# Placing layernorm and transposes of two row chunks a few matmul groups earlier in a fused transformer block, and requesting their input earlier

## The chip, the cores and the metric

The kernel runs on one core of a Trainium2 chip. The metric is the device time of one execution in microseconds (us). A profiled execution also has a span (first to last instruction), which is about 2 us shorter than the device time. The mean granted TensorE clock, as a share of the full clock, is 1.000 except where the text says otherwise.

Engines are named as in the profile: PE is TensorE (matmul), PEld its weight load, DVE VectorE, ACT ScalarE, POOL GpSimd, SP the engine that issues every DMA of this kernel (SPq is its sequencer). Line L178 is a helper through which nearly every instruction is recorded, so groups are told apart by their tiles, `out<-in`.

## The reference

One sequence of 2048 rows, width 1024: an adaptive layernorm, linear attention with 32 heads, then a SwiGLU feed-forward with hidden width 3584, both with residuals.

```
mod = silu(c) @ w_mod -> sa, ca, ga, sb, cb, gb
h = layernorm(x) * (1 + ca) + sa
q, k, v = split(h @ wqkv);  pq, pk = phi(q), phi(k)      # phi(t) = (t+1 if t>0 else exp(t)) + 1e-6
o = (pq @ (pk^T v)) / (pq . sum(pk) + 1e-6)
x = x + ga * (o @ wo)
h = layernorm(x) * (1 + cb) + sb
x = x + gb * ((silu(h @ w_gate) * (h @ w_up)) @ w_down)
```

Only the first layernorm and the q and k projections matter here, about the first 130 us.

## The kernel before

The program is a list of operations; each engine takes its own in list order, and semaphore waits are derived from the data. The 2048 rows are four chunks of 512 (four tiles of 128 rows). For chunk `ch` TensorE computes 8 k groups and 8 q groups of 8 matmuls each. ScalarE and VectorE then empty the group's PSUM bank (the memory that TensorE writes to); this is called evacuation. Work for the *next* chunks is hung between these groups: `add(s1, g, f)` puts `f` behind group `g` of chunk 1, `s2` is chunk 2, `kside` the k half of chunk 0.

```python
HT = T("ht", 120 * KB, [128, 2, NDT, 512], BF16)   # two buffers: chunk ch uses ch % 2

def ln1_stats_ops(st): ...   # VectorE: 2 x bn_stats (0.64 us), 1 x bn_aggr, per 128-row tile
def ln1_rstd(ch): ...        # VectorE, then POOL pow
def ln1_xn(st): ...          # VectorE: x = (x - mean) * rstd, in place, 0.46 us
def th_dma(st): ...          # SP: DMA transpose of the tile into HT (one per tile)
def th_mod(ch, dt):          # scale and shift one of 8 slices of the transposed chunk, in place
    if dt % 2 == 0 or ch == 1: P.dve("tensor_scalar", out=HT[:, ch % 2, dt, :], ...)   # 0.40 us
    else:                      P.act("activation",    out=HT[:, ch % 2, dt, :], ...)   # 0.82 us

def chunk(ch, side):
    for gi in range(16):
        if gi < 8: k_group(ch, gi)       # 8 matmuls reading HT[:, ch % 2, 0..7, :], then
        else:      q_group(ch, gi - 8)   # phi_evac: ACT exp and relu; DVE min/add and sum, in pairs
        for f in side.get(gi, []): f()

# chunk 2 (tiles 8..11), prepared during chunk 1
for i in range(4): add(kside, i, lambda i=i: x_load(8 + i))          # request x
for i, f in enumerate(ops8_11): add(s1, (i * 5) // 12, f)            # 12 statistics operations
add(s1, 4, lambda: ln1_rstd(2))
for jj in range(4):
    add(s1, 6 + jj // 2, lambda jj=jj: ln1_xn(8 + jj))
    add(s1, 6 + jj // 2, lambda jj=jj: th_dma(8 + jj))
for i, dt in zip([10, 11, 11, 12, 12, 13, 13, 14], range(8)): add(s1, i, lambda dt=dt: th_mod(2, dt))
# chunk 3 (tiles 12..15)
for i in range(4): add(s1, 2 * i, lambda i=i: x_load(12 + i))
for i, f in enumerate(ops12_15): add(s1, 8 + (i * 7) // 12, f)
add(s1, 15, lambda: ln1_rstd(3))
for jj in range(4):
    add(s2, 1 + jj, lambda jj=jj: ln1_xn(12 + jj)); add(s2, 1 + jj, lambda jj=jj: th_dma(12 + jj))
for dt in range(8): add(s2, 7 + dt, lambda dt=dt: th_mod(3, dt))
# ... cut: modulation rows (macc, 1.2 us each on VectorE, chunk 2 groups 4..11), attention, feed-forward
```

(Shortened: `ops8_11` and `ops12_15` stand for lists built in loops.)

## Time and profile before

Before: 839.48 us (median of 4 runs, 839.27 to 839.64).

| of the profiled execution | |
|---|---|
| span | 837.6 us |
| TensorE busy | 99% |
| TensorE's waits after 27 us that the change can reach | two shown, 1.20 and 0.44 us |

The page's busy times and its chain of waits say that TensorE's order of work is the time:

```profile
PE 827.7 (99%) x4113; PEld 380.2 (45%) x4113; DVE 306.1 (37%) x673; ACT 203.0 (24%) x355; POOL 41.1 (5%) x52
PE 91%; DVE 4%; SPq 2%; DMA 2%; issue 1%; ACT 0%; DVEq 0%; ACTq 0%
```

TensorE's timeline from the end of start-up to the 16 small matmuls after chunk 3's third k group. Columns: start, duration, engine, line, operation, `out<-in`, shapes, count, and in brackets the idle time before and what ended it. Consecutive equal instructions are merged.

```profile
26.83 49.34 PE L178 MATMUL ps<-ht,wqk 128*128 128x512 bf16 x226
77.37 27.80 PE L178 MATMUL ps<-ht,wqk 128*128 128x512 bf16 x128 [1.20 <-DVE ht L178]
105.61 4.06 PE L178 MATMUL ps<-ht,wqk 128*128 128x512 bf16 x18 [0.44 <-DVE ht L178]
109.50 0.54 PE L178 MATMUL ps<-ones,mhl 128*128 128x1 bf16 x16
```

Two stops are shown, while chunk 2 and chunk 3 begin. Both end when a scale step (`ht<-ht`) is done. Rows of VectorE's timeline (its first and last scale step for chunk 2, then for chunk 3), of ScalarE's (first and last for chunk 2), and of the issuing engine's:

```profile
71.59 0.41 DVE L178 TENSOR_SCALAR ht<-ht,modcol 128x512 bf16<-128x512 bf16 x1 [4.73 <-DMA ht<-xres]
76.91 0.41 DVE L178 TENSOR_SCALAR ht<-ht,modcol 128x512 bf16<-128x512 bf16 x1
94.57 0.41 DVE L178 TENSOR_SCALAR ht<-ht,modcol 128x512 bf16<-128x512 bf16 x1 [1.50 <-DMA ht<-xres]
105.15 0.40 DVE L178 TENSOR_SCALAR ht<-ht,modcol 128x512 bf16<-128x512 bf16 x1
```

```profile
71.57 0.81 ACT L178 ACTIVATE ht<-ht,modcol 128x512 bf16<-128x512 bf16 x1 [2.71 <-DMA ht<-xres]
76.56 0.84 ACT L178 ACTIVATE ht<-ht,modcol 128x512 bf16<-128x512 bf16 x1
```

```profile
60.82 2.70 SPq L178 DMA_TRANSPOSE ht<-xres  x2
63.57 3.34 SPq L178 DMA_TRANSPOSE pk_90<-pkt_75  x1
66.95 2.69 SPq L178 DMA_TRANSPOSE ht<-xres  x2
```

Chunk 2's four transposes leave SP at 60.8 to 68.3 us, two of them behind a larger transpose. The trace has the last one landed at 71.47. Until then VectorE and ScalarE both stand idle (4.73 and 2.71 us), each in front of its first scale step. They finish their last scale steps at 77.32 and 77.40. For chunk 3 VectorE waits 1.50 us for the transposes and ends its last scale step at 105.55, just before TensorE goes on at 105.61.

### The profile page before, as it was taken

The page shows a single profiled execution, that of the slowest core. Times are in us where ns is not written, and L with a number is a line of the kernel's source. Part 1 is how long each engine was busy: PE and PEld are TensorE (multiplying, and loading weights), DVE is VectorE, ACT ScalarE, POOL GpSimd, SP SyncE. Part 2 cuts the span into 40 slices and gives each one's busy share as a digit, 9 for nine tenths or more (in the row PEclk, how much of TensorE's full clock was granted, in tenths as well). Part 3 has the DMA queues.
Part 4 walks back from the last instruction along what each step waited for, and adds up shares of the span by engine and source line. Part 5 has one row for each costly group of instructions (what it writes and reads, how often), then busy time and mean ns, then how long its engine had stood idle before and what let it go on. Part 6 is the DMA issues. An engine that isn't in the chain of part 4 may idle for free.

```text
span 837.6 us, 10117 instructions
## 1 busy us (share of the span) xinstructions
PE 827.7 (99%) x4113; PEld 380.2 (45%) x4113; DVE 306.1 (37%) x673; ACT 203.0 (24%) x355; POOL 41.1 (5%) x52
## 2 busy tenths in 40 slices
PE   8999999999999999999999999999999999999998
PEld 4444444444444444444444444444444444444444
DVE  5797886656974222111221112022221112111111
ACT  4666753223333111110111111021111111111111
POOL 1000000000050000030000003000000300000000
PEclk9999999999999999999999999999999999999999
DMA  9987753847096895530355562045557104553000
GB/s 279 263 191 187 187 152 139 185 124 278 24 251 191 257 306 153 154 70 26 113 150 151 151 162 59 19 114 151 151 151 182 44 13 114 151 153 98 1 25 26
DMA packets 195085, 117.18 MB, mean 140 GB/s; under 512 B 49624, under 2 KB 178784, under 8 KB 195040
## 3 DMA queue, kind: packets, MB, share of 16 engines
q1 hardware_dynamic: 195040, 116.55, 51.2%
q8 instruction: 32, 0.52, 0.3%
q14 instruction: 13, 0.11, 0.0%
HBM read 100.67 MB, written 4.33 MB: 125 GB/s over the span
## 4 chain that ended last, share of the span: by engine, by line
PE 91%; DVE 4%; SPq 2%; DMA 2%; issue 1%; ACT 0%; DVEq 0%; ACTq 0%
PE ps L178 91%; SPq L178 2%; DVE acc L178 1%; DMA wsa<-in_w_mod_dram 1%; DMA ht<-xres 1%; DVE xres L178 0%; DVE stats L178 0%; DVE pqt L178 0%; DVE ht L178 0%; DVE e_94 L178 0%; DVE mhl L178 0%; DVE pkt_75 L178 0%; ACT e_94 L178 0%; ACT mw L178 0%; DVE mv L178 0%
## 5 line engine op out<-in xcount | busy, mean ns | idle before, releaser
L178 DVE TENSOR_TENSOR at<-sg,ps 128x512 bf16<-128x512 bf16 x112 | 77.0, 687 | 296.2 <-PE ps L178 296.2
L178 ACT ACTIVATE sg<-ps 128x512 bf16<-128x512 f32 x112 | 66.9, 597 | 310.3 <-PE ps L178 310.3
L178 PE MATMUL ps<-ht,wqk 128*128 128x512 bf16 (+1 forms) x522 | 112.8, 375 | 2.4 <-DVE ht L178 2.2
L178 PE MATMUL ps<-wd_a,at 128*128 128x512 bf16 (+2 forms) x528 | 113.5, 373 | 0.0
L178 PE MATMUL ps<-wd_b,at 128*128 128x512 bf16 (+2 forms) x396 | 85.8, 373 | 0.0
L178 PEld LDWEIGHTS ps<-ht,wqk 128*128 128x128 bf16 x522 | 50.2, 98 | 62.8 <-DVE ht L178 4.0
L178 PEld LDWEIGHTS ps<-wd_a,at 128*128 128x128 bf16 x528 | 51.1, 98 | 59.8
L178 DVE TENSOR_TENSOR ut<-att,gb_b 128x512 bf16<-128x512 bf16 (+1 forms) x32 | 13.8, 433 | 167.3 <-ACT att L178 167.3
L178 ACT ACTIVATE att<-ps 128x512 bf16<-128x512 f32 (+1 forms) x32 | 17.4, 591 | 182.1 <-PE ps L178 182.1
L178 PEld LDWEIGHTS ps<-wd_b,at 128*128 128x128 bf16 x396 | 38.3, 98 | 44.6
L178 PE MATMUL ps<-mw,pqt 128*128 128x512 bf16 x256 | 56.2, 379 | 0.1
L178 PE MATMUL ps<-h2t,gug_116 128*128 128x512 bf16 x224 | 52.9, 379 | 0.0
L178 PE MATMUL ps<-h2t,gug_114 128*128 128x512 bf16 x224 | 52.9, 379 | 0.0
L178 PE MATMUL ps<-h2t,guu_118 128*128 128x512 bf16 x224 | 52.9, 379 | 0.0
L178 PE MATMUL ps<-h2t,guu_119 128*128 128x512 bf16 x224 | 52.9, 379 | 0.0
L178 PE MATMUL ps<-h2t,guu_120 128*128 128x512 bf16 x224 | 52.9, 379 | 0.0
L178 PE MATMUL ps<-h2t,gug_113 128*128 128x512 bf16 x224 | 52.9, 379 | 0.0
L178 PE MATMUL ps<-h2t,guu_117 128*128 128x512 bf16 x224 | 52.9, 379 | 0.0
L178 PE MATMUL ps<-h2t,gug_115 128*128 128x512 bf16 x224 | 52.9, 379 | 0.0
L178 POOL TENSOR_SCALAR h2t<-h2t,modcol 128x512 bf16<-128x512 bf16 x32 | 28.4, 902 | 393.9 <-DMA h2t<-xn_121 377.6
L178 ACT ACTIVATE e_94<-ps 128x512 bf16<-128x512 f32 x64 | 39.3, 614 | 26.3 <-PE ps L178 20.3
L178 ACT ACTIVATE rl<-ps 128x512 bf16<-128x512 f32 x64 | 39.3, 614 | 0.0
(116 smaller groups left out, 632.5 us busy)
## 6 DMA issues: line engine op xcount, KB each, us to landing
gug_113<-in_B_w_gate_dram SPq DMA_DIRECT2D x14, 512.0 KB, 4.0
guu_117<-in_B_w_up_dram SPq DMA_DIRECT2D x14, 512.0 KB, 5.3
gug_114<-in_B_w_gate_dram SPq DMA_DIRECT2D x14, 512.0 KB, 4.1
guu_118<-in_B_w_up_dram SPq DMA_DIRECT2D x14, 512.0 KB, 5.4
gug_115<-in_B_w_gate_dram SPq DMA_DIRECT2D x14, 512.0 KB, 4.0
guu_119<-in_B_w_up_dram SPq DMA_DIRECT2D x14, 512.0 KB, 5.4
gug_116<-in_B_w_gate_dram SPq DMA_DIRECT2D x14, 512.0 KB, 4.0
guu_120<-in_B_w_up_dram SPq DMA_DIRECT2D x14, 512.0 KB, 5.3
```

Source lines behind the costliest of these rows:

```text
L178: return getattr(e, method)(**kw)
```

## The change

The intent is to have chunk 2's and chunk 3's input transposed well before it is scaled, so that TensorE meets finished slices. Of the 16 groups of a chunk, chunk 2's normalisation and transposes move from groups 6 and 7 to group 2; chunk 3's normalisation moves from groups 1 to 4 of chunk 2 to groups 13 and 14 of chunk 1, its transposes to group 0 of chunk 2. No operation is added or removed. The core of the diff:

```diff
+        for st in range(8, 12):          # at the start, behind the last weight tile
+            x_load(st)
...
-        for i in range(4):
-            add(kside, i, lambda i=i: x_load(8 + i))
...
         q_phase_chunk0(qside)
+        for st in range(12, 16):
+            x_load(st)
...
-        for i in range(4):
-            add(s1, 2 * i, lambda i=i: x_load(12 + i))
...
-        ops = []
         for jj in range(4):
-            ops += ln1_stats_ops(8 + jj)
-        for i, f in enumerate(ops):                       # statistics, tiles 8..11
-            add(s1, (i * 5) // 12, f)
-        add(s1, 4, lambda: ln1_rstd(2))
+            for f in ln1_stats_ops(8 + jj):
+                add(s1, jj // 2, f)
+        add(s1, 1, lambda: ln1_rstd(2))
         for jj in range(4):
-            add(s1, 6 + jj // 2, lambda jj=jj: ln1_xn(8 + jj))
-            add(s1, 6 + jj // 2, lambda jj=jj: th_dma(8 + jj))
-        for i, dt in zip([10, 11, 11, 12, 12, 13, 13, 14], range(NDT)):
+            add(s1, 2, lambda jj=jj: ln1_xn(8 + jj))
+            add(s1, 2, lambda jj=jj: th_dma(8 + jj))
+        for i, dt in zip([10, 10, 11, 11, 12, 12, 13, 13], range(NDT)):
             add(s1, i, lambda dt=dt: th_mod(2, dt))
...
         for i, f in enumerate(ops):                       # statistics, tiles 12..15
-            add(s1, 8 + (i * 7) // 12, f)
-        add(s1, 15, lambda: ln1_rstd(3))
+            add(s1, 8 + (i * 5) // 12, f)
+        add(s1, 12, lambda: ln1_rstd(3))
         for jj in range(4):
-            add(s2, 1 + jj, lambda jj=jj: ln1_xn(12 + jj))
-            add(s2, 1 + jj, lambda jj=jj: th_dma(12 + jj))
+            add(s1, 13 + jj // 2, lambda jj=jj: ln1_xn(12 + jj))
+            add(s2, 0, lambda jj=jj: th_dma(12 + jj))
         for dt in range(NDT):
-            add(s2, 7 + dt, lambda dt=dt: th_mod(3, dt))
+            add(s2, 6 + dt, lambda dt=dt: th_mod(3, dt))
```

(The remarks behind `#` were added for this text.)

## The prediction

> **What bounds it.** The table of busy time gives TensorE 827.7 of 837.6 us (99%) at clock 1.0; the chain of waits runs through TensorE for 91%. So only TensorE's idle time (about 10 us) can be won. The waits of TensorE show 4.4 us for early loads (before 27 us) and 2.2 us on VectorE for the transposed activations (ht), 0.60 us of that before 15 us. The timeline of TensorE shows just two gaps the change can reach: 1.20 us at 76.2-77.4 (chunk 2 starts) and 0.44 us at 105.2-105.6 (chunk 3 starts). Ceiling: 1.64 us, 0.2%.
>
> **Why these gaps exist.** Chunk 2's four transposes are issued at 60.8 to 68.3 us and the last lands near 71.5; VectorE sits idle 4.73 us for it (66.9-71.6), then does its scale steps (0.40 us) between normalisation statistics (0.68 us) and finishes the seventh slice at 77.3. At chunk 3 VectorE waits 1.50 us for the transposes (landed 94.5), then works through the 1.3 us accumulation steps and finishes at 105.55.
>
> **What the change does.** It adds and removes no operation. Chunk 2: statistics (8 x 0.64 us plus aggregation) now run in groups 0 and 1, normalisation (4 x 0.46 us) and transposes right after. From 49.7 us on VectorE: 5.4 us statistics, 1.6 us evacuation, about 1.1 us waiting for POOL's power, 1.8 us normalisation; transposes issued near 58-60, landed near 65-66 instead of 71.5, ahead of their use at about 68. The 4.7 us stall goes, and VectorE's work before chunk 2 (23 us) ends at about 74-75 against TensorE's need near 75-76. Chunk 3: transposes go out when chunk 1's last matmul frees the buffer (about 76) and land by about 83, used from about 87; that stall goes as well. I expect both gaps to close: -1.6 us.
>
> **What it may cost.** (a) The x tiles of chunk 2 (1 MB) are now ahead of chunk 1's transposes in the one DMA queue. The Trainium skill ("DMA: Bandwidth & Descriptors", section "Queues, rings and completion order") says each DMA engine consumes descriptors in ring order; the trace's landings follow issue order here. One MB takes 3.0 us in this stage (the last weight tile, 1 MB, lands 3.1 us after the previous one). The first two transposes should land near 40-41 instead of 37.5-38.3, but the stretch 38-40 us shows DMA at 0, so the last two (landed 42.4, 43.6) move little: estimate 0 to 0.8 us. Chunk 1's scale steps start at 43.83 and end at 48.1 with almost no slack, so a delay goes into a new gap at the start of chunk 1. I count 0.3 us. (b) VectorE lags some 7 us during chunk 1; four evacuation buffers and five PSUM banks should hide that.
>
> **Sum.** 839.4 - 1.64 + 0.3 = 838.1 us; range 837.4 to 839.4. Faster by over 2%: 0.5%; within 2%: 99%; slower: 0.5%.
>
> **What would show it.** Right: no TensorE gap near 76 and 105 us; VectorE without the 4.7 and 1.5 us waits for transposes; chunk 2's transposes landed before 68 us; TensorE waiting on VectorE falls from 2.2 to about 0.6 us, plus any gap near 48 us. Step (a) wrong: a TensorE gap above 0.6 us near 48 us and chunk 1's last transpose landing after 44.5. Step (b) wrong: TensorE idle between 50 and 75 us, or VectorE's last scale step of chunk 2 still after 76.
>
> **What would make it wrong.** (a) at a microsecond or more; (b); the queue blocked behind a transpose that waits for its buffer.

## The result, and the profile after

The changed kernel took 837.0 us (median of 4 runs, 836.42 to 837.5), 2.48 us less than before. The ratio is 0.997 with a 95% interval of 0.9953 to 0.9988. Ratios here are the mean time of one kernel's fast runs over that of the other's of the same rounds, so not quite the ratio of the medians quoted. The direction and the mechanism were as predicted; the size was not: 837.0 lies below the predicted range of 837.4 to 839.4. The profiled span fell from 837.6 to 835.5 us, by 2.1 us.

The chain of waits, then the timelines of TensorE, VectorE, ScalarE and the issuing engine after the change, for the same places:

```profile
PE 96%; SPq 2%; DVE 1%; DMA 1%; issue 0%; ACT 0%; DVEq 0%
```

```profile
27.00 80.56 PE L178 MATMUL ps<-ht,wqk 128*128 128x512 bf16 x372
107.40 0.54 PE L178 MATMUL ps<-ones,mhl 128*128 128x1 bf16 x16
```

```profile
68.83 0.40 DVE L178 TENSOR_SCALAR ht<-ht,modcol 128x512 bf16<-128x512 bf16 x1
74.93 0.40 DVE L178 TENSOR_SCALAR ht<-ht,modcol 128x512 bf16<-128x512 bf16 x1
100.40 0.40 DVE L178 TENSOR_SCALAR ht<-ht,modcol 128x512 bf16<-128x512 bf16 x1
```

```profile
67.47 0.81 ACT L178 ACTIVATE ht<-ht,modcol 128x512 bf16<-128x512 bf16 x1 [0.17 <-DMA ht<-xres]
72.46 0.84 ACT L178 ACTIVATE ht<-ht,modcol 128x512 bf16<-128x512 bf16 x1
```

```profile
59.02 5.37 SPq L178 DMA_TRANSPOSE ht<-xres  x4
64.43 3.06 SPq L178 DMA_TRANSPOSE pk_89<-pkt_74  x1
```

The same 372 matmuls (226 + 128 + 18 before) are now one unbroken row. Chunk 2's transposes leave together from 59.0 us and the last lands at 67.37 instead of 71.47. Both engines finish their scale steps ahead of TensorE. The margin is thin for chunk 2: VectorE ends its last scale step at 75.33 us and the matmul that reads the slice starts at 75.89. For chunk 3 the two times are 100.80 and 103.52.

Here is the number that the prediction missed. From the first of these matmuls to the first small one, the timelines give 109.50 - 26.83 = 82.67 us before and 107.40 - 27.00 = 80.40 us after. The change took 2.27 us out of this stage alone, not 1.64. Start-up cost 0.17 us more in this profile, which leaves the 2.1 us of the spans.

Why did the brackets show only 1.64? They give idle time between the *end* of one matmul and the start of the next. A matmul's row lasts 0.379 us, but in a stream the next one starts 0.216 us after it. So each stop is 0.379 - 0.216 = 0.16 us longer than its bracket, and stops below 0.16 us show as none at all. Counting from start to start, in excess of 0.216 us, the trace of before has:

```
start us   start to start   excess   idle shown
 28.23        0.328          0.11       0.00
 75.78        0.499          0.28       0.12  (hidden in the merged row x226)
 77.37        1.589          1.37       1.20
105.61        0.819          0.60       0.44
```

The last three sum to 2.26 us, and none of them is left after. The 0.11 us stop at 28 us is there in both. The Trainium skill, "TensorE: Matmul & The Clock Gate", section "Part 2: What happens when you issue a matmul", says that one matmul's drain overlaps the next one's fill, so that the spacing is the streaming time and not the latency. This trace agrees with its 216 ns: the start-to-start time over 300 to 800 us is 0.216 in the median. The brackets have to be read with that in mind.

### The profile page after: what moved, and what is told of

Read it like the earlier page. It is cut to its first block, busy times and chain, and to the rows that moved or that the text cites. A ratio compares the mean times of both kernels' runs of the same rounds, so it can differ in the third digit from the quotient of the medians.

```text
span 835.5 us, 10117 instructions
## 1 busy us (share of the span) xinstructions
PE 827.6 (99%) x4113; PEld 380.4 (46%) x4113; DVE 306.0 (37%) x673; ACT 203.4 (24%) x355; POOL 41.1 (5%) x52
## 4 chain that ended last, share of the span: by engine, by line
PE 96%; SPq 2%; DVE 1%; DMA 1%; issue 0%; ACT 0%; DVEq 0%
PE ps L178 96%; SPq L178 2%; DMA wsa<-in_w_mod_dram 1%; DVE acc L178 0%; DVE xres L178 0%; DVE mhl L178 0%; ACT mw L178 0%; DVE ve_72 L178 0%; DVE ut L178 0%; DVE mean_70 L178 0%; DVE msq_71 L178 0%; DVE sumx L178 0%; DVEq L249 0%
```

## The experiments

All are the kernel before or the changed kernel with one thing moved; all outputs were correct. "Excess" is the start-to-start time beyond 0.216 us, summed over the stop named. (In eight of the eleven traces a matmul record is missing about every fiftieth time and leaves an interval of 0.43 us with 0.05 us of idle time shown; those are left out.) The runs came in three batches with 9 or 10 runs of the kernel before each; their means are 839.63, 839.60 and 839.46 us. The first two batches, on one chip, share nine of these runs; the third (change third time, late transposes filled, x later in time) ran on another chip.

| run | mean us | difference to before | ratio, 95% interval |
|---|---|---|---|
| change again | 837.23 | -2.40 | 0.9958 to 0.9983 |
| change, third time | 837.29 | -2.17 | 0.9961 to 0.9988 |
| requests only | 839.24 | -0.39 | 0.9982 to 1.0007 |
| chunk 2 only | 838.36 | -1.26 | 0.9971 to 0.9999 |
| chunk 3 only | 840.18 | +0.56 | 0.9994 to 1.0019 |
| order only | 838.52 | -1.08 | 0.9974 to 1.0001 |
| all x early | 840.76 | +1.16 | 1.0 to 1.0026 |
| statistics after scale | 842.97 | +3.37 | 1.0024 to 1.0052 |
| late transposes | 844.27 | +4.67 | 1.0043 to 1.0067 |
| late transposes, filled | 842.58 | +3.12 | 1.0024 to 1.005 |
| x later, in time | 837.24 | -2.22 | 0.9961 to 0.9986 |

### 1. The change again, twice

No edit. First:

> The changed kernel itself, timed again to size the gain and its scatter. Theory A (the whole gain is three TensorE stops taken away at the starts of chunks 2 and 3; counted as the time from one matmul's start to the next beyond the usual 0.216 us they are 0.28 + 1.37 + 0.60 = 2.26 us): 2.0 to 2.5 us less than before, and no such stop between 30 and 130 us. If the gain here is well above 2.5 us or below 1.7 us, something besides these stops is at work.

It measured -2.40 us. Third time, later:

> The changed kernel once more, as the yardstick in the same rounds as the next two: 2.2 to 2.5 us faster than before, mean clock 1.000 in every run because no stop of TensorE is left in chunks 1 to 3.

It measured -2.17 us (slightly under the expected 2.2) with clock 1.000 in all five runs. Together with the first result (-2.48 by medians) the gain is 2.2 to 2.5 us, in line with 2.26 us of stops. Nothing beyond the stops has to be assumed. One detail: in the first of these profiles 0.29 us of small stops (0.08 to 0.11 each) stand near 48 us, where chunk 1 begins; in the result's own profile and in the third there are none.

### 2. The requests without the order

The diff's four `x_load` hunks only.

> Kernel before with only the x requests moved as in the change; the order of VectorE's work is that of before. Theory A (order of layernorm and transposes does it): within 0.4 us of before, the stops near 76 and 105 us stay (about 1.6 and 0.6 us of excess). Rival B (part of the gain, the 0.2 to 0.4 us by which the timed gain exceeds the stops, or more, comes from earlier x requests and less DMA traffic between the transposes): 0.4 to 1 us faster, with transposes of chunk 2 landing clearly before 71 us.

It measured -0.39 us with an interval that holds zero. The stops stayed: 1.26 us near 78 and 0.67 us near 106, and 0.50 us of small stops came near 48 us. By themselves the requests show no gain. (The traced execution is the slowest of the five, 840.59 us against 838.43 to 839.29, so its stops may not be those of the others.)

### 3. Chunk 2 alone, chunk 3 alone

Only the hunks of tiles 8 to 11, and only those of tiles 12 to 15; requests as before.

> Kernel before with only chunk 2's statistics, normalisation, transposes and scale steps placed as in the change; chunk 3 and the x requests as before. Theory A: the stops near 76 us go (1.66 us of excess), the one near 105 us (0.60 us) stays, so about 1.6 us faster than before. If the stops share one cause, the third goes too and it is 2.2 us faster.

> Kernel before with only chunk 3's statistics, normalisation, transposes and scale steps placed as in the change; chunk 2 and the x requests as before. Theory A: the stop near 105 us goes (-0.60 us), but three more statistics operations (about 1.4 us, of which about 0.6 us fits in VectorE's wait for the transposes) now stand before chunk 2's last scale step, so the stop near 76 us grows by 0.5 to 1 us: between 0.2 us faster and 0.4 us slower than before. If the two parts are independent: 0.6 us faster.

Chunk 2 alone: -1.26 us by means (-1.39 by medians, -1.4 in the profiled span). The stops near 76 us are gone and the one near 105 stays, grown from 0.60 to 0.71 us, so it does not follow from the first. Chunk 3 alone: the stop near 105 us is gone, but those at 76 to 78 us grew from 1.66 to 2.10 us, as expected from the statistics that now stand before chunk 2's scale steps. The parts are not additive: chunk 3's part gains nothing without chunk 2's. The mean of +0.56 us was a bit worse than expected. Three of its five runs, at clock 1.000, took 839.31 to 839.83 us, as before; the two at mean clock 0.998 took 840.91 and 841.36. Experiment 7 follows that up.

### 4. The order without the requests

All hunks except the `x_load` ones.

> The change without its x requests: both chunks' layernorm, transposes and scale steps placed as in the change, x requested where before had it. Theory A (the order does it, not the requests): faster by 1.7 to 2.5 us as the full change is, with no stop of TensorE near 76 and 105 us and none of the small ones near 48 us that two runs with early x requests showed (0.3 and 0.5 us in all); if the last two x tiles now land after VectorE wants them, a stop of at most 0.5 us near 76 us. Rival B (the requests carry part of it): faster by less than 1.5 us.

It measured -1.08 us: half the gain is missing, as rival B said. VectorE's and TensorE's timelines show why:

```profile
70.36 1.29 DVE L178 BATCH_NORM_STATS2 stats<-xres 128x6 f32<-128x512 bf16 x2 [1.56 <-DMA xres<-in_A_x_dram]
76.54 3.63 PE L178 MATMUL ps<-ht,wqk 128*128 128x512 bf16 x16 [0.83 <-DVE ht L178]
```

The x tiles 14 and 15 were issued only at 67.0 us, behind the big transposes in SP's one queue. Tile 14 landed at 70.34. VectorE, in order, waited 1.56 us for it with chunk 2's scale steps behind. The stop at 76.5 us (0.99 us of excess) is back, twice the half microsecond that had been allowed for it. (Another 0.32 us stood at 33.7 us, where TensorE waited for a weight tile.) So the requests show no gain of their own, but the new order needs the later half of them.

### 5. Both halves of x at the start

```diff
-        for st in range(8, 12):
+        for st in range(8, 16):
             x_load(st)
...
-        for st in range(12, 16):
-            x_load(st)
```

> The change with x of chunk 3 requested at the start too, another 1 MB ahead of chunk 1's transposes. Step (a) of the prediction (slack of about 2 us in the queue, used up by the first MB): chunk 1's last transpose lands 1.5 to 3 us later than 43.8, a stop of TensorE of 1.5 to 2.5 us opens near 48 us, and the gain shrinks to between 0.7 us and nothing. If the queue has still slack, the gain stays at 2.2 us or more.

The trace's landings of chunk 1's four transposes, in us:

```
                      1st     2nd     3rd     4th    x ahead of them
before               37.55   38.33   42.39   43.58    none
changed              40.38   41.25   42.59   43.80    1 MB
all x early          42.96   43.83   45.18   46.58    2 MB
```

The first MB delays the first two transposes by 2.8 and 2.9 us and the last two, which wait for VectorE anyway, by 0.2 us. The second MB moves all four by 2.6 to 2.8 us. This is what the prediction said of the slack, with the mechanism it took from the Trainium skill, "DMA: Bandwidth & Descriptors", section "Queues, rings and completion order": on each DMA engine the descriptors of one queue are consumed in order. The landings in the table agree: in each run they come in the order of issue, behind the x tiles. TensorE's timeline pays at once:

```profile
47.27 1.27 PE L178 MATMUL ps<-ht,wqk 128*128 128x512 bf16 x4 [0.27 <-DVE ht L178]
50.10 60.24 PE L178 MATMUL ps<-ht,wqk 128*128 128x512 bf16 x263 [1.56 <-DVE ht L178]
```

The stops sum to 2.7 us of excess near 48 us, and the whole gain is lost and more: +1.16 us. The expectation of "0.7 us to nothing" of gain was too good by over a microsecond. A part of that is the stops themselves: even the two runs at clock 1.000 (839.75 and 840.19 us) were 0.2 and 0.6 us slower than before. In the other three the stop was followed, as the trace of one of them shows, by something that had not been in any account: eight matmuls at about 0.43 us instead of 0.216. The record of the granted clock has 0.5 for 3.41 us there.

### 6. VectorE's order or the transposes?

A rival for the stop at 76 us: chunk 3's statistics stand between chunk 2's scale steps on VectorE.

```diff
-            add(s1, 8 + (i * 7) // 12, f)
+            add(s1, 14 + i // 6, f)
```

> Kernel before with one thing moved: chunk 3's twelve statistics operations stand behind chunk 2's scale steps (groups 14 and 15) and not between them. The transposes of chunk 2 still land near 71.5 us. Rival C (the stop at 76 us is VectorE's order: statistics between the scale steps): last scale step done near 74.5, no stop near 76, the one near 105 stays (0.6 us or somewhat more): 1.3 to 1.7 us faster than before. Theory A in its narrow form (the late transposes alone make the stop): the stop near 76 us stays above 1 us and the time is that of before.

The rival fell. VectorE was done with its last scale step of chunk 2 at 75.7 us instead of 77.3 (1.2 us later than expected), yet the stop stayed. TensorE's timeline, and the ScalarE row that ends the first stop:

```profile
77.28 27.15 PE L178 MATMUL ps<-ht,wqk 128*128 128x512 bf16 x123 [1.07 <-ACT ht L178]
105.36 0.60 PE L178 MATMUL ps<-ht,wqk 128*128 128x512 bf16 x2 [0.92 <-DVE ht L178]
107.95 2.74 PE L178 MATMUL ps<-ht,wqk 128*128 128x512 bf16 x6 [1.99 <-DVE ht L178]
```

```profile
76.39 0.84 ACT L178 ACTIVATE ht<-ht,modcol 128x512 bf16<-128x512 bf16 x1
```

The releaser is now ScalarE. It had stood 2.50 us before its first scale step, until the last transpose landed at 71.29, with its own evacuations piling up behind, and it reached the eighth slice at 76.39. A profile names only the releaser that came last; here a second one stood 0.1 us behind it. Relieving VectorE alone gave 1.31 us of excess instead of 1.66. That points to the landing of the transposes, which feeds both engines; the opposite edit below tests it. The price came at chunk 3: statistics later, transposes later (last landed 96.8 instead of 94.5), stops of 1.08 and 2.15 us at 105 to 108 us, and again half-speed matmuls behind them.

The opposite edit keeps the change and issues only chunk 2's transposes late:

```diff
-            add(s1, 2, lambda jj=jj: th_dma(8 + jj))
+            add(s1, 6 + jj // 2, lambda jj=jj: th_dma(8 + jj))
```

> The change with one thing undone: chunk 2's transposes are issued after groups 6 and 7 as before, though their input is ready as early as in the change. They should land near 71 to 72 us again and VectorE wait for them. Both A (narrow) and the joint cause (late transposes with statistics standing between the scale steps behind them) want a stop of 1 to 2.5 us near 76 us and a gain of 0 to 1.2 us; if VectorE's order alone counted, the gain would stay at 2.2 us or more.

The stop came, and far larger than expected. VectorE waited 5.40 us, the last transpose landed at 73.91 (2.4 us later than before, as the larger transposes in the queue are later in this order), and TensorE stopped four times: first for a PSUM bank, then for scale steps. The first bracket below names VectorE, but the kernel lets only ScalarE read these banks; ScalarE stood 7.04 us in front of its first scale step and ended its next evacuation at 75.81, just before TensorE went on. TensorE's timeline:

```profile
75.95 0.59 PE L178 MATMUL ps<-ht,wqk 128*128 128x512 bf16 x2 [1.51 <-DVE e L178]
77.17 0.60 PE L178 MATMUL ps<-ht,wqk 128*128 128x512 bf16 x2 [0.63 <-DVE ht L178]
78.15 0.60 PE L178 MATMUL ps<-ht,wqk 128*128 128x512 bf16 x2 [0.38 <-DVE ht L178]
80.61 9.67 PE L178 MATMUL ps<-ht,wqk 128*128 128x512 bf16 x43 [1.86 <-DVE ht L178]
```

The excess is 5.0 us. So the change's front-loaded VectorE work is only good with its early transposes; the order and the transposes are one measure. The shift of the scale steps by one place, which is also in the diff, was never tried alone, and no part of chunk 3's half was.

### 7. What a stop costs beyond itself

Sorting the runs by the mean clock of the core shows a second cost. Spans in us:

| run | clock 1.000 | clock 0.998 | clock 0.996 |
|---|---|---|---|
| chunk 3 only | 837.3, 837.5, 837.8 | 838.9, 839.3 | |
| all x early | 837.8, 838.1 | 838.6, 839.5, 839.8 | |
| statistics after scale | 839.4 | 841.0, 841.1, 841.5, 841.6 | |
| late transposes | 840.2 | | 841.9, 842.5, 842.7, 842.7, 843.5 |

One 3.41 us stretch at half clock in 837 us is a mean clock of 1 - 0.5 x 3.41 / 837 = 0.998, and two give 0.996. The means by class differ by 1.3 to 1.9 us for one stretch and 2.5 us for two, against 1.7 us of lost work in a stretch (3.4 in two; but late transposes have only one run at 1.000 to compare with). Four more kernels have one run at 0.998 each, and there the excess over the same kernel's mean at 1.000 is smaller: 0.5 us (before), 0.4 (chunk 2 only), 1.0 (order only) and 0.5 (late transposes, filled). So a stretch does not always cost 1.3 us or more. Of these four runs only the last was traced (its stretch lies at start-up, below). In the traced run of "statistics after scale" the windows show the clock (columns: window, length, then busy us of PE, PEld, DVE, ACT and POOL with counts, granted clock, DMA share, GB/s):

```profile
104.00:108.00 4.00, 1.09 (x6) 0.17 (x4) 4.00 (x12) 2.76 (x5) 0.00 (x0) 0.98 0.14 8
108.00:112.00 4.00, 3.78 (x11) 1.46 (x13) 3.00 (x7) 1.13 (x3) 0.00 (x0) 0.59 0.98 356
112.00:116.00 4.00, 4.00 (x34) 2.03 (x33) 1.81 (x6) 2.26 (x5) 0.00 (x0) 1.00 0.44 164
```

TensorE is busy for 1.09 of the 4 us from 104 to 108 us and then gets half the clock for 3.41 us from 107.9 (0.59 in the mean of the next window). To test the cause, the late-transposes kernel was given 21 useless matmuls into an unused PSUM bank, at the places of its stops (4.5 us of work into 5.0 us of stops). Their results are never read.

```diff
+            fill = {0: 7, 2: 3, 4: 2, 6: 9} if (ch, nt) == (2, 0) else {}
             for dt in range(NDT):
+                for _ in range(fill.get(dt, 0)):
+                    P.pe("matmul", out=PS[:, 6, :], lhsT=IDENT[:], rhs=WQK[:, 0, 0:512], start=True, stop=True)
```

> The run with chunk 2's transposes late again, plus 21 matmuls into an unused PSUM bank (21 x 0.216 = 4.5 us) placed into the stops that its trace shows near 76 to 81 us (5.0 us in all). Theory: its typical time (844.5, mean clock 0.996) is made of the stops (5.0 us) and of stretches at half clock that the stops bring on (5 of its 6 runs; the one run at clock 1.000 took 842.15). With TensorE kept busy the clock stays at 1.000 and the time is 841.5 to 842.8 in all runs, 2 us less though more work is done. If the half clock is unrelated to TensorE's idle time: clock 0.996 again and about 844.5.

It is 1.69 us faster than without the useless matmuls (842.58 against 844.27 mean, on different chips in batches whose kernels before differ by 0.14), with the clock at 1.000 in four of five runs. The windows of the traced run, which is the fifth, show full clock at the filled place and a half-clock stretch at start-up, away from it:

```profile
24.00:28.00 4.00, 4.00 (x42) 2.00 (x41) 0.11 (x2) 0.00 (x0) 0.00 (x0) 0.69 1.05 343
76.00:80.00 4.00, 4.00 (x20) 1.63 (x18) 3.93 (x14) 4.00 (x8) 0.10 (x1) 1.00 1.02 362
80.00:84.00 4.00, 4.00 (x20) 1.70 (x19) 4.00 (x13) 3.79 (x8) 0.91 (x1) 1.00 0.43 105
```

This fits the theory that the half clock comes from TensorE's idle time, but does not prove it: the kernel without the useless matmuls was not run again on that chip, and its one traced run (842.15 us) kept clock 1.000 through all its stops, so where the half-clock stretches of the others lay was not seen. What supports the theory are the traces of experiments 5 and 6, where the stretch begins at 51.3 and 107.9 us, right at the stops. Two of the five runs (843.03 and 843.09) were slightly over the expected 842.8, one of them the one with the start-up stretch.

The Trainium skill, "TensorE: Matmul & The Clock Gate", section "Part 1: The HAM clock gate (the "warmup" mystery)", describes a monitor that halves the array's clock after an idle window of about 3.4 us and says that this window runs freely. The length agrees (3.41 us in the clock's record) and a freely running window would fit the chance in it: one kernel, some runs with and some without. The stops in front of it here are shorter than that window; the closing list comes back to this.

Does this explain part of the change's gain? Of 19 runs of the kernel before whose clock is listed, one is at 0.998; of the changed kernel's 14, none. That is too few to count it, and the 2.26 us of stops do not leave room for much.

### 8. Is the early request needed?

The change costs up to 0.3 us near 48 us in some executions, because x of chunk 2 stands ahead of chunk 1's transposes. A version with the change's order, x of chunk 2 where before had it, and x of chunk 3 after the first group of chunk 1:

```diff
-        for st in range(8, 12):
-            x_load(st)
...
+        for i in range(4):
+            add(kside, i, lambda i=i: x_load(8 + i))
...
-        for st in range(12, 16):
-            x_load(st)
...
+        for i in range(4):
+            add(s1, 0, lambda i=i: x_load(12 + i))
```

> The change's order with x of chunk 2 requested where before had it (behind chunk 1's transposes) and x of chunk 3 all at once after the first group of chunk 1. If only chunk 3's request mattered (the run with the order alone lost about 1 us to x tiles 14 and 15 that landed at 70 and 71 us), no stop near 76 us, none of the small ones near 48 us, and a time equal to the change or up to 0.3 us less. If the early request of chunk 2 is needed, a stop returns and it is slower than the change by 0.5 us or more.

It measured 837.24 us against 837.29 for the change in the same rounds: the same. Its trace has no stop between 29 and 107 us. Only chunk 3's request had to move, and not as far. A gain of 0.3 us could not have been told from the scatter (837.1 to 837.54 for the change), so neither version is shown to beat the other.

## Why the prediction was wrong

- *What bounds it* held: only TensorE's stops could be won, and they were.
- *"Ceiling: 1.64 us"* is the step that failed. The two stops were right, but their size was taken from the idle time shown. Counted from start to start they measure 1.37 + 0.60 us, and a third of 0.28 us was hidden in a merged row: 2.26 us. The runs measured 2.2 to 2.5 us.
- *The cost (a)*, "I count 0.3 us", was the second wrong term. Its mechanism was right: the first two of chunk 1's transposes landed at 40.4 and 41.3 us (predicted 40 to 41), the last at 43.80 instead of 43.58. But the slack took it all in the result's own profile, and 0 to 0.3 us in the three profiles of the change. With 2.26 and 0 to 0.3 the same sum gives 837.1 to 837.4 us, against 837.0, 837.36 and 837.18 measured in the medians. All three lie below the range that the sum with 1.64 had led to.
- *"I expect both gaps to close"* held, and so did the times of the way there: transposes issued from 59.0 us (predicted 58 to 60); last landed at 67.4, later than the predicted 65 to 66 but before the 68 us named as a test; VectorE's last scale step of chunk 2 done at 75.3 (predicted 74 to 75, tested against 76); the waits of 4.73 and 1.50 us gone. Chunk 3's transposes were issued from 75.8 us and landed by 83.4 (predicted 76 and 83). TensorE's waits for VectorE on `ht` fell from 2.2 to 0.6 us, as named.
- *Why these gaps exist* was incomplete: it named VectorE alone. ScalarE was just as late (77.40 against 77.32 us), which experiment 6 brought out.
- *Cost (b)* held: VectorE lagged in chunk 1 (it began the second pair of evacuations at 60.27 us instead of 55.27) and TensorE did not stop between 50 and 75 us.

What stays open: where the half-clock stretches lay in runs that were not traced (one of before, one each of "chunk 2 only" and "order only"); whether requests alone gain a few tenths; which of chunk 3's moves closed its stop; and whether the half clock of the late transposes goes away on one and the same chip when the stops are filled.

## What to carry to other kernels

When a saturated TensorE is the bound, measure its stops from matmul start to matmul start: with pipelined matmuls the shown idle time is short by the overlap, here 0.16 us per stop, and small stops vanish. Before relieving the engine that a wait names, look whether another engine was waiting for the same source and would be the next to be late; move the source. And treat a stop of 1.5 to 2 us on TensorE as possibly dearer than its length: in experiments 5 and 6 stops of 1.7 and 2.2 us, each with a smaller one before it, had 3.4 us at half clock behind them. Filling the stops with useless matmuls seemed to avoid that; not having the stop is better.

## What the Trainium skill lacked or had wrong

- "TensorE: Matmul & The Clock Gate", section "HAM oscillation — how this bites in real kernels", gives as the rule no idle gap above about 3.4 us; the page's next section adds, without lengths, that frequent short idle times do it too. Here shorter ones were enough when they came close together: half clock for 3.41 us followed stops of 0.4 and 1.7 us within 3 us (experiment 5), and of 1.1 and 2.2 us (experiment 6). They were not always enough: the traced run with late transposes had stops of 1.7, 0.8, 0.5 and 2.0 us within 7 us at clock 1.000.
- The same page, section "Back-to-back issue gap", says that in a real stream of weight load and matmul pairs N=512 runs at about 131 ns, and that 216 ns over-counts. In this kernel, which is such a stream, the median start-to-start is 216 ns over 500 us.
- "Perfetto Trace Analysis", section "Optimization Strategy", advises to find the gaps between slices. The page warns that busy time misleads because matmuls are pipelined, but it doesn't say that a gap between matmul rows is short by the overlap of two rows: 1.64 us shown, 2.26 us real.
- The page "DMA: Bandwidth & Descriptors" gives bandwidths for DMA transposes, but no time from issue to landing for one of 128 x 1024 bf16 (256 KB): here it took 3.24 and 3.15 us with little else in the queue (issued 39.15 and 40.43, landed 42.39 and 43.58 us before).
